# Attention pieces spaced 10 and 18 instead of 14, inverse columns counted at 3.0 instead of 4.5, and MoE 1's low parts on GpSimd

## The chip, the cores and the metric

The kernel runs on one core of a Trainium2 chip. Its five engines have queues of their own that run in order: TensorE (PE, with weight loads listed apart as PEld), VectorE (DVE), ScalarE (ACT), GpSimd (POOL) and SyncE (SP), which issues transfers. An instruction that waits for a semaphore holds up all that stands behind it on its engine. The metric is the device time of one execution in microseconds, lower is better.

## The reference

Three stages follow each other: a delta-rule attention, a MoE layer without a nonlinearity (a product of two projections), and a second layer with a leaky ReLU of learned slope. All is in float32.

```python
# attention: 4 batches x 8 heads, 768 steps, head size 48
k_n = k / (norm(k) + 1e-06)
for t in range(S):
    y[:, :, t] = einsum('bhd,bhde->bhe', q[:, :, t], state)
    v_old = einsum('bhde,bhd->bhe', state, kt)
    state = state + bt * einsum('bhd,bhe->bhde', kt, vt - v_old)
# x: 3072 tokens x 384
x = ((x @ w_a) * (x @ w_b)) @ w_out                      # MoE 1, d_ff 1536
h = x @ w_in                                             # MoE 2, d_ff 2048
out = (maximum(h, 0) + alpha * minimum(h, 0)) @ w_out2
```

## The kernel before, in words

**Attention** is done in six chunks of 128 time steps (`c` = 0 to 5), each in two halves of 64 (`j`). Within a chunk the recurrence is solved by inverting a triangular matrix for each of 32 (half, head pair) tiles. VectorE does that inverse by substitution: it transposes the matrix (line 287), then adds thirty *columns*, two instructions each, a multiply into `itmp` (line 303) and an add into `eu` (line 304). Each column needs the one before it. The result is transposed twice at the start of the chunk that uses it: into `hw` (line 311) and into `TT` (line 315), and ScalarE copies part of TT (line 319).

On TensorE a chunk is a series of *pieces*. First three pieces of `offdiag` (products `w` and `xx`, lines 337 and 353, kept by ScalarE into `hw` and `TT`), then for each half `step`: two each of `rp`, `up`, `sp` and `yp`. Beside the `up` and `sp` pieces of the first half stand the key products of the *next* chunk (line 220, "mates", whose result VectorE masks into `ef`, line 253), and beside those of the second half its query products. When the last key product is masked, behind the second `sp` of the first half, `keys_done` begins the next chunk's inverse. It goes on in the background and has to be finished before the next chunk's first piece, since `w` reads `hw`.

**MoE 1** of chunk c - 1 fills TensorE between the pieces of chunk c. It is a generator (`moe1`) that yields once for each 128x128x512 product, 324 steps a chunk: up projections `p` (line 640) into two banks, whose product `a` (line 595) VectorE forms, and down projections `o` (line 642). For accuracy each float32 operand is *split* into a high part (a ScalarE cast, line 538) and a low part (a subtraction, line 539), and each product is made of three passes. The weight of a step (`wu`) is split shortly ahead of use by `prepare`, three ahead; the low part goes to VectorE or GpSimd by a string, `LO` while weights are still being decoded, `STEADY` afterwards and `LAST` once MoE 2's weights are being decoded. The low parts of `g` are always GpSimd's (line 604).

**The order** is written out by the program as it is built. `run(moe, n, start)` puts n MoE steps between two pieces and moves a count `now` on by one a step, and by `PIECE` = 5 for the piece. `FILLS[c]` is that n. The inverse goes on through `leisurely`: it puts the next column into VectorE's queue whenever VectorE's booked time `until[DVE]` has been reached by `now`; each column books 4.5 + (31 - m) m / 100 counts (line 298; 1.7 in place of 4.5 for chunk 1's inverse, which lies in PSUM). What has not been placed by the end of the chunk is placed at once by `finish(inv)`, behind the splits of `x`, the chunk's result. So these counts decide only in which order instructions stand in a queue; on the chip each waits for what it needs.

After the last `yp` of a chunk the MoE steps are run down to 16, the result is transposed and split into `x` (lines 458 and 539), 10 more steps end the chunk's MoE, and the next chunk starts with 17 steps beside the two transposes (`DIAGONAL` = 8, 4, 5).

Chunk 0 runs before MoE 1 starts. In chunk 1 MoE 1's weights are decoded from the form in which they arrive, on all of ScalarE, VectorE and GpSimd (lines 500 to 510). Chunk 5 has no next inverse; there, from its first `rp` on, MoE 2's weights are decoded. After chunk 5 the rest of MoE 1 runs, then MoE 2.

Of the kernel before, what the change touches and what calls it, by code (L numbers as in the profile page):

```python
# [22 lines left out]
ACT, DVE, POOL, SP = "act", "dve", "pool", "sp"  # L23
# [5 lines left out]
SLACK = 0.5  # L29

PIECE = 5
FILLS = (0, 13, 14, 14, 14, 14)

AHEAD, WAIT = 6, 21
DIAGONAL = (8, 4, 5)
# [23 lines left out]
XAHEAD = 32  # L59


LO = "ppppppv"
STEADY = "ppppv"
LAST = "ppv"

STAGES = [("u", 4), ("g", 2), ("r", 2), ("w6", 1), ("w7", 1), ("w8", 1)]
# [14 lines left out]
class Attention:  # L81
# [198 lines left out]
    def inverting(s, L, room=None):  # L280

        nc, ap = s.nc, s.ap
        a0 = ap.tile([128, 32, 32], F32, tag="eu", name="eu", bufs=1)
        nc.vector.transpose(a0, L["ef"][:, :, 0:32].rearrange("p a t -> p t a"))
        s.spend(DVE, 9)
        yield
        nc.vector.memset(a0.rearrange("p t s -> p (t s)")[:, 0:1024:33], 1.0)  # L290
        eu = L["eu"] = a0
        if room is not None:
            eu = L["eu"] = room
            nc.scalar.copy(eu, a0)
        yield
        tmp = ap.tile([128, 256], F32, tag="itmp", name="itmp", bufs=1)
        for m in range(1, 31):
            s.spend(DVE, (1.7 if room is not None else 4.5) + (31 - m) * m / 100)
            nt = 31 - m
            a = eu[:, m : m + 1, 0:m].to_broadcast([128, nt, m])  # L300
            b = a0[:, m + 1 : 32, m : m + 1].to_broadcast([128, nt, m])
            tm = tmp[:, : nt * m].rearrange("p (t s) -> p t s", s=m)
            nc.vector.tensor_tensor(tm, a, b, ALU.mult)  # L303
            nc.vector.tensor_tensor(eu[:, m + 1 : 32, 0:m], eu[:, m + 1 : 32, 0:m], tm, ALU.add)  # L304
            yield
# [160 lines left out]
def attn_moe_kernel(tc, kt, qt, kn, vn, beta, w_a, w_b, w_o, w_in, w_o2, alpha, out):  # L466
    nc = tc.nc
    with ExitStack() as ctx:
# [13 lines left out]
        def bank(name, tag):  # L482
            return pools[tag].tile([128, 512], F32, tag=tag, name=name, bufs=BANKS[tag])
# [49 lines left out]
        def xroom(kk, c, shape, dt, name):  # L533
            return xp.tile([128, *shape], dt, tag=f"x{kk}{c % 2}", name=name)

        def split(dst, src, eng=nc.gpsimd):

            nc.scalar.copy(dst[:, 0], src)  # L538
            eng.tensor_tensor(dst[:, 1], src, f32(dst[:, 0]), ALU.subtract)  # L539
            spend(ACT, 2)  # L540
            if eng is nc.vector:
                spend(DVE, 2.2)
            else:
                spend(POOL, 4.5)
# [20 lines left out]
        def prepare():  # L565
# [3 lines left out]
            if m is not None:  # L569
# [3 lines left out]
                ready.append(gp.tile([128, 2, DM], F32R, tag="u", name="wu", bufs=NU))  # L573
                lo = LO if left or line else STEADY
                if len(wanted) < 2 * M2:
# [96 lines left out]
        def run(it, n, start=0):  # L672

            nonlocal now
            more = True
            now += start
            for _ in range(n):
                more = more and next(it, "end") is None
                now += 1
                for b in list(background):  # L680
                    if next(b, "end") == "end":
                        background.remove(b)
            return more

        def leisurely(inv):

            while True:
                if until[DVE] <= now and next(inv, "end") == "end":
                    return
                yield  # L690

        def finish(b):
            for _ in b:
                pass
            background[:] = [x for x in background if x is not b]
# [23 lines left out]
        room = p0.tile([128, 32, 32], F32, tag="inv", name="inv")  # L719
# [71 lines left out]
        def decoding(depth):  # L791
            while left or line:
                decode1(depth)
                yield
# [34 lines left out]
        def decoding2(depth):  # L829
            while wanted or line:  # L830
                rooms = spare if len(wanted) <= len(spare) else free
                if len(wanted) > keep[0] and rooms and len(line) < depth:
                    begin(line, weight2(*wanted.pop(0), rooms.pop(0)))
                else:
                    advance(line)
                yield
# [59 lines left out]
        moe = moe1()  # L896
        for c in range(NSC):

            going = c > 0
            fill = FILLS[c]  # L900
            if c > 0:
                N = A.load(c + 1) if c + 1 < NSC else None
                if c == 1:
                    finish(inv)
                    diagonal = A.diagonal(L)
                    now = max(now, until[DVE])
                    background.append(decoding(DEPTH))
                    run(moe, WAIT)
                    for _ in diagonal:
                        run(moe, 1)  # L910
                    early_ctx.close()
                    pools["out"] = ctx.enter_context(tc.tile_pool(name="psm", bufs=1, space=PSUM))
                    going = run(moe, AHEAD) and going
                else:
                    for n, _ in enumerate(A.diagonal(L)):
                        run(moe, DIAGONAL[n])
                tag = "chain" if c == 1 else "pre"
                for i, _ in enumerate(A.offdiag(L, tag)):
                    going = run(moe, fill, PIECE) and going
                    if N is not None:  # L920
                        if i == 1:
                            norms = A.norms(N)
                        if i > 0:
                            next(norms)
                mates = [[None, None], [None, None]]

                def keys_done():
                    nonlocal inv
                    A.fold(N, 1)
                    inv = A.inverting(N)  # L930
                    background.append(leisurely(inv))
                    A.scale_keys(N)

                if N is not None:
                    after = {(0, 8): lambda: A.fold(N, 0), (1, 8): keys_done}
                    for q in range(2):
                        mates[q] += [A.mate(N, *jg, tag, q == 1, after.get(jg) if q == 0 else None, c > 1) for jg in HALF]
                closed.clear()
                L["y"] = [None, None]
                for j in range(2):  # L940
                    for i, _ in enumerate(A.step(c, j, L, mates[j])):
                        if N is not None and i == j == 0:
                            next(norms, None)
                            A.masks(N, 0)
                            A.masks(N, 1)
                        going = run(moe, fill, PIECE) and going
                        if c == NSC - 1 and i == j == 0:
                            rooms2.append(rooms1.pop())
                            background.append(decoding2(DEPTH2))
                        if N is not None and i == 3:  # L950
                            A.load_values(c + 1, N)
                    keep[0] = 2 * M2 - KEEP
                    if N is not None and j == 0:
                        A.scale_values(N, 0)
                if N is not None:
                    A.scale_values(N, 1)
                while togo[0] > AHEAD1:
                    run(moe, 1)
                X[c] = []
                for kk in range(KT):  # L960
                    X[c].append(xroom(kk, c, [2, 512], F32R, "x"))
                    split(X[c][-1], A.transposed(L["y"], kk, xp=bank("xp", "pre" if kk == 2 else "chain")), nc.vector)
                    run(moe, min(2, togo[0]))
                run(moe, togo[0])
                if N is not None:
                    finish(inv)
            else:
                x1 = [bank("x1", "ab") for _ in range(2)]
                for kk in range(KT):
                    at = kk % 2 * 256  # L970
                    A.transposed(L["y"], kk, (1,), x1[kk // 2], at)
                    split(xs[kk][:, :, 256:], x1[kk // 2][:, at : at + 256], nc.vector)
                while len(ready) < LEAD:
                    prepare()
            L = N
# [53 lines left out]
        going, ahead = True, XAHEAD - 3  # L1029
        while going or background:  # L1030
            going = run(moe, 9)
# [96 lines left out]
```

## Time and profile before

| | us |
|---|---|
| median of 3 runs | 1156.25 (1155.47 to 1157.4) |
| profiled execution | 1155.86, of which span 1154.1 |
| TensorE busy | 1048.2 (91%) |
| VectorE busy | 672.7 (58%) |
| GpSimd busy | 555.9 (48%) |
| ScalarE busy | 467.3 (40%) |
| chain that ended last | TensorE 69%, VectorE 16%, ScalarE 6%, GpSimd 4% |

The stages, in us from the start of the span: chunk 0 and its preparation to about 110, chunk 1 to 235, chunks 2, 3, 4 and 5 at some 109 each (their first `w` at 242.5, 351.4, 460.3 and 568.8), the rest of MoE 1 to 745, MoE 2 to the end at full speed of TensorE. Busy shares over the whole span hide that the stages have different limits: VectorE is busy 7 tenths of the time up to 670 and 4 tenths behind it. What a chunk is worth is read inside the chunk.

### The profile page before, as it was taken

How to read it: one execution, taken by the hardware profiler on the slowest of the kernel's cores; microseconds unless marked ns; L12 is line 12 of the kernel's file. 1: busy time of each engine (PE TensorE's matmuls, PEld its weight loads, DVE VectorE, ACT ScalarE, POOL GpSimd, SP SyncE). 2: the span in 40 equal slices, each digit the busy share in tenths (PEclk: the TensorE clock that was granted, in tenths of full speed). 3: DMA queues.
4: the chain of work that ended last, by engine and by line, in shares of the span. 5: the costliest groups of instructions: out<-in, count | busy, mean ns of one | idle time of the engine just before them, and what ended most of it. 6: DMA issues, size and time to landing. Idle time of an engine off the chain costs nothing.

```text
span 1154.1 us, 23828 instructions
## 1 busy us (share of the span) xinstructions
PE 1048.2 (91%) x10048; PEld 885.1 (77%) x10048; DVE 672.7 (58%) x1085; ACT 467.3 (40%) x903; POOL 555.9 (48%) x467
## 2 busy tenths in 40 slices
PE   6277898779998997999799999999999999999997
PEld 5165686567776776777677887799999999999997
DVE  7787577755774579468737468734343433434332
ACT  4273664554345433643456577511221121122211
POOL 6255588736463644554447678632223333333222
PEclk8577998889998999999899999999999999999999
DMA  9215132500030021000024144010202001020101
GB/s 266 79 30 165 52 108 64 151 29 16 15 83 29 16 66 33 30 16 15 4 75 119 39 137 133 24 50 1 56 1 55 1 8 48 1 56 1 28 1 28
DMA packets 25596, 61.42 MB, mean 53 GB/s; under 512 B 4496, under 2 KB 7568, under 8 KB 25488
## 3 DMA queue, kind: packets, MB, share of 16 engines
q1 hardware_dynamic: 25168, 59.50, 17.8%
q8 instruction: 79, 1.29, 0.5%
q10 hardware_dynamic: 320, 0.39, 0.1%
q14 instruction: 29, 0.24, 0.1%
HBM read 50.44 MB, written 9.44 MB: 52 GB/s over the span
## 4 chain that ended last, share of the span: by engine, by line
PE 69%; DVE 16%; ACT 6%; POOL 4%; issue 3%; DMA 1%; ACTq 0%; POOLq 0%; DVEq 0%
PE h L551 17%; PE p L640 17%; PE o L1009 17%; PE o L642 10%; DVE itmp L303 4%; DVE eu L304 2%; DVE inv L304 1%; PE rp L408 1%; PE yp L447 1%; DVE v L827 1%; PE up L421 1%; POOL W L510 1%; DVE hw L311 1%; ACT wu L538 1%; PE g L220 1%
## 5 line engine op out<-in xcount | busy, mean ns | idle before, releaser
L640 PE MATMUL p<-x,wu 128*128 128x512 f32 x1296 | 332.5, 401 | 11.4 <-DVE a L595 6.3
L640 PEld LDWEIGHTS p<-x,wu 128*128 128x128 f32 x1296 | 241.3, 191 | 67.0 <-issue 7.9
L539 POOL TENSOR_TENSOR wu<-W,wu 128x384 fp32r<-128x384 f32 x166 | 177.7, 1074 | 203.6 <-ACT wu L538 186.1
L539 POOL TENSOR_TENSOR g<-neg,g 128x512 fp32r<-128x512 f32 x95 | 123.2, 1297 | 276.8 <-ACT g L538 276.8
L1009 PE MATMUL o<-v,g 128*128 128x384 f32 x1152 | 217.8, 337 | 0.2 <-ACT g L538 0.2
L551 PE MATMUL h<-x,v 128*128 128x512 f32 x864 | 215.2, 393 | 0.0
L1009 PEld LDWEIGHTS o<-v,g 128*128 128x128 f32 x1152 | 204.6, 188 | 9.2 <-ACT g L538 0.6
L1000 DVE TENSOR_SCALAR neg<-h,al 128x512 f32<-128x512 f32 (+1 forms) x97 | 72.3, 745 | 218.1 <-PE h L551 217.3
L538 ACT CAST g<-neg 128x512 fp32r<-128x512 f32 (+1 forms) x97 | 59.7, 615 | 325.6 <-DVE neg L1001 315.5
L551 PEld LDWEIGHTS h<-x,v 128*128 128x128 f32 x864 | 160.7, 188 | 29.3
L642 PE MATMUL o<-g,wu 128*128 128x512 f32 x648 | 178.7, 412 | 1.3 <-DVE TT L315 0.6
L642 PEld LDWEIGHTS o<-g,wu 128*128 128x128 f32 x648 | 124.4, 197 | 30.1 <-DVE wu L539 1.0
L538 ACT CAST wu<-W 128x384 fp32r<-128x384 f32 x216 | 108.7, 512 | 46.8 <-POOL W L510 23.4
L604 POOL TENSOR_TENSOR g<-a,g 128x512 fp32r<-128x512 f32 x71 | 95.4, 1344 | 40.8 <-ACT g L599 40.8
L595 DVE TENSOR_TENSOR a<-p,a 128x512 f32<-128x512 f32 x72 | 49.4, 686 | 65.3 <-PE p L640 29.4
L539 DVE TENSOR_TENSOR wu<-W,wu 128x384 fp32r<-128x384 f32 x50 | 52.0, 1040 | 59.6 <-ACT wu L538 58.3
L599 ACT CAST g<-a 128x512 fp32r<-128x512 f32 x72 | 44.5, 618 | 84.6 <-DVE a L595 84.3
L220 PE MATMUL g<-Z 48*64 48x64 f32 x768 | 61.8, 241 | 13.8 <-DMA Z<-in_kt_dram 7.0
L304 DVE TENSOR_TENSOR eu<-eu,itmp 128x30 f32<-128x30 f32 (+14 forms) x120 | 68.9, 575 | 4.1
L1001 DVE SCALAR_TENSOR_TENSOR neg<-h,neg 128x512 f32<-128x512 f32 (+1 forms) x97 | 66.5, 686 | 3.3
L220 PEld LDWEIGHTS g<-Z 48*64 48x64 f32 x768 | 55.9, 153 | 14.7 <-DMA Z<-in_kt_dram 6.8
L303 DVE TENSOR_TENSOR itmp<-eu 128x30 f32<-128x30 f32 (+14 forms) x120 | 65.3, 544 | 2.8
(101 smaller groups left out, 1284.6 us busy)
## 6 DMA issues: line engine op xcount, KB each, us to landing
v<-in_w_in_dram SPq DMA_DIRECT2D x16, 384.0 KB, 3.4
v<-in_w_o_dram SPq DMA_DIRECT2D x16, 384.0 KB, 3.8
k<-in_kn_dram SPq DMA_DIRECT2D x6, 768.0 KB, 5.0
Z<-in_kt_dram SPq DMA_DIRECT2D x24, 192.0 KB, 5.8
Z<-in_qt_dram SPq DMA_DIRECT2D x24, 192.0 KB, 6.7
v<-in_vn_dram SPq DMA_DIRECT2D x12, 384.0 KB, 3.3
raw<-in_w_a_dram SPq DMA_DIRECT2D x12, 384.0 KB, 5.7
raw<-in_w_b_dram SPq DMA_DIRECT2D x12, 384.0 KB, 6.1
```

Of the source, the lines that this page charges most:

```text
L220: nc.tensor.matmul(g[0:64, i, :], Z[64:112, 0, i8 + i, :], Z[64:112, a, i8 + i, :], start=True, stop=True)
L303: nc.vector.tensor_tensor(tm, a, b, ALU.mult)
L304: nc.vector.tensor_tensor(eu[:, m + 1 : 32, 0:m], eu[:, m + 1 : 32, 0:m], tm, ALU.add)
L538: nc.scalar.copy(dst[:, 0], src)
L539: eng.tensor_tensor(dst[:, 1], src, f32(dst[:, 0]), ALU.subtract)
L551: nc.tensor.matmul(p, u[:, a, kk * 128 : kk * 128 + 128], xs[kk][:, b], start=(n == 0), stop=(n == 3 * KT - 1))
L604: (nc.vector if last else nc.gpsimd).tensor_tensor(g[m][:, 1], a[m], f32(g[m][:, 0]), ALU.subtract)
L640: nc.tensor.matmul(ab[m, t], wu, X[c][kk][:, q], start=(n == 0), stop=(n == 8))
L642: nc.tensor.matmul(o[kk], wu, g[m][:, q], start=(m == 0 and n < 3), stop=(m == M1 - 1 and n > 5),)
L1000: nc.vector.tensor_scalar(t[:, cs], h[:, cs], 0.0, al[:, m : m + 1], ALU.min, ALU.mult)
L1001: nc.vector.scalar_tensor_tensor(t[:, cs], h[:, cs], 0.0, t[:, cs], ALU.max, ALU.add)
L1009: nc.tensor.matmul(o[n], g[:, a, n * 128 : n * 128 + 128], V[m][1][:, b], start=(m == 0 and i == 0), stop=(m == M2 - 1 and i == 2),)
```

## The change

Four numbers and two strings are altered.

- `FILLS` has two numbers for each chunk. The first is the number of MoE steps behind the three `offdiag` pieces and the first six pieces of half 0 (`rp`, `up`, `sp`, two each), that is until the next inverse begins; the second stands behind all later pieces. Chunks 2 to 4 had 14 throughout and now have 10 and 18; chunk 1 had 13 and has 11 and 14; chunk 5 had 14 and has 13 and 14.
- A column of an inverse in SBUF books 3.0 instead of 4.5 counts (plus the same second term).
- `LO` and `STEADY` are "p": every low part of MoE 1's weights is GpSimd's until `LAST` applies. VectorE has 21 low parts of `wu` instead of 50.

```diff
-FILLS = (0, 13, 14, 14, 14, 14)
+FILLS = ((0, 0), (11, 14), (10, 18), (10, 18), (10, 18), (13, 14))
...
-LO = "ppppppv"
-STEADY = "ppppv"
+LO = "p"
+STEADY = "p"
 LAST = "ppv"
...
         for m in range(1, 31):
-            s.spend(DVE, (1.7 if room is not None else 4.5) + (31 - m) * m / 100)
+            s.spend(DVE, (1.7 if room is not None else 3.0) + (31 - m) * m / 100)
...
-            fill = FILLS[c]
+            fill, fill2 = FILLS[c]
...
-                        going = run(moe, fill, PIECE) and going
+                        going = run(moe, fill if j == 0 and i < 6 else fill2, PIECE) and going
```

VectorE's queue at the end of chunk 2, before. The rows are the last columns that stand ahead of the splits of `x`, the splits, and the first of nine columns behind them; `hw` follows behind the ninth.

```order
L595 TENSOR_TENSOR a<-p,a 128x512
L303 TENSOR_TENSOR itmp<-eu 128x220
L304 TENSOR_TENSOR eu<-eu,itmp 128x11x20
L303 TENSOR_TENSOR itmp<-eu 128x210
L304 TENSOR_TENSOR eu<-eu,itmp 128x10x21
L539 TENSOR_TENSOR x<-xp,x 128x512 x3
L595 TENSOR_TENSOR a<-p,a 128x512
L539 TENSOR_TENSOR wu<-W,wu 128x384
L303 TENSOR_TENSOR itmp<-eu 128x198
L304 TENSOR_TENSOR eu<-eu,itmp 128x9x22
```

The same place in VectorE's queue now:

```order
L303 TENSOR_TENSOR itmp<-eu 128x58
L304 TENSOR_TENSOR eu<-eu,itmp 128x2x29
L303 TENSOR_TENSOR itmp<-eu 128x30
L304 TENSOR_TENSOR eu<-eu,itmp 128x30
L595 TENSOR_TENSOR a<-p,a 128x512
L539 TENSOR_TENSOR x<-xp,x 128x512 x3
L595 TENSOR_TENSOR a<-p,a 128x512
L311 STREAM_TRANSPOSE hw<-eu 128x32x32
L315 STREAM_TRANSPOSE TT<-eu 128x32x32
```

The column of 30 is the last one. It now stands ahead of `x`, in chunks 3 and 4 too; in chunk 1 three columns still stand behind `x`, where there were eleven.

ScalarE's queue at the start of chunk 2, before, from the copies of TT to the second copies of `hw`:

```order
L319 COPY TT<-TT 32x32x32
L592 COPY a<-p 128x512
L319 COPY TT<-TT 32x32x32
L342 COPY hw<-w 32x512 x2
L538 CAST wu<-W_543 128x384
L599 CAST g<-a 128x512
L651 COPY x2s<-o_2896 128x512
L651 COPY x2s<-o_2897 128x512
L651 COPY x2s<-o_2898 128x512
L538 CAST wu<-W_555 128x384
L342 COPY hw<-w 32x512 x2
```

And now:

```order
L319 COPY TT<-TT 32x32x32
L592 COPY a<-p 128x512
L319 COPY TT<-TT 32x32x32
L342 COPY hw<-w 32x512 x2
L538 CAST wu<-W_543 128x384
L599 CAST g<-a 128x512
L651 COPY x2s<-o_2896 128x512
L651 COPY x2s<-o_2897 128x512
L651 COPY x2s<-o_2898 128x512
L342 COPY hw<-w 32x512 x2
L358 COPY TT<-xx 32x16x32 x2
```

One weight cast has moved behind the second copies of `hw`; the rest of the stretch is the same.

## Rows read from the trace of the kernel before

**Rows 1.** Busy time by stage (chunk 1, chunk 2); columns as its first line.
```profile
core 0: us, PE busy (x) PEld busy (x) DVE busy (x) ACT busy (x) POOL busy (x), PEclk, DMA share, GB/s
121.00:232.00 111.00, 94.73 (x1117) 73.58 (x1116) 78.87 (x134) 64.82 (x131) 82.58 (x73) 0.92 0.33 97
341.00:450.00 109.00, 101.85 (x1361) 81.84 (x1360) 73.75 (x122) 47.86 (x92) 53.61 (x45) 0.97 0.14 38
```

**Rows 2.** TensorE in order of time: start, us, what, [idle before, releaser]; four `w`.
```profile
242.51 0.71 PE L337 MATMUL w<-hw,ef 32*32 32x32 f32 x19 [7.42 <-DVE hw L311]
...
351.44 1.92 PE L337 MATMUL w<-hw,ef 32*32 32x32 f32 x64 [7.15 <-DVE hw L311]
...
460.34 0.28 PE L337 MATMUL w<-hw,ef 32*32 32x32 f32 x3 [6.98 <-DVE hw L311]
...
568.79 0.34 PE L337 MATMUL w<-hw,ef 32*32 32x32 f32 x5 [6.36 <-DVE hw L311]
```

**Rows 3.** TensorE in order of time, pieces that follow boundaries 1, 2 and 4.
```profile
258.08 0.25 PE L408 MATMUL rp<-SU,Z 48*64 48x48 f32 x1
...
358.02 0.22 PE L353 MATMUL xx<-TT,hw 32*32 32x32 f32 x2
...
362.63 1.20 PE L353 MATMUL xx<-TT,hw 32*32 32x32 f32 x64
363.76 2.33 PE L642 MATMUL o<-g,wu 128*128 128x512 f32 x9
...
367.16 0.25 PE L408 MATMUL rp<-SU,Z 48*64 48x48 f32 x1
...
585.04 0.25 PE L408 MATMUL rp<-SU,Z 48*64 48x48 f32 x1
```

**Rows 4.** VectorE in order of time, boundary 2.
```profile
338.96 0.68 DVE L595 TENSOR_TENSOR a<-p,a 128x512 f32<-128x512 f32 x1
...
349.27 2.02 DVE L311 STREAM_TRANSPOSE hw<-eu 128x1024 f32<-128x1024 f32 x1
351.14 1.90 DVE L315 STREAM_TRANSPOSE TT<-eu 128x1024 f32<-128x1024 f32 x1
```

**Rows 5.** VectorE in order of time, boundary 1 and boundary 3.
```profile
229.74 0.68 DVE L595 TENSOR_TENSOR a<-p,a 128x512 f32<-128x512 f32 x1
...
238.87 0.25 DVE L303 TENSOR_TENSOR itmp<-eu 128x84 f32<-128x84 f32 x1
...
240.39 1.97 DVE L311 STREAM_TRANSPOSE hw<-eu 128x1024 f32<-128x1024 f32 x1
...
449.62 0.67 DVE L595 TENSOR_TENSOR a<-p,a 128x512 f32<-128x512 f32 x1
```

**Rows 6.** ScalarE in order of time, start of chunk 2.
```profile
353.07 1.04 ACT L319 COPY TT<-TT 32x1024 f32<-32x1024 f32 x1 [8.63 <-DVE TT L315]
...
355.69 1.18 ACT L342 COPY hw<-w 32x512 f32<-32x512 f32 x2
...
359.94 1.17 ACT L342 COPY hw<-w 32x512 f32<-32x512 f32 x2
...
367.14 0.23 ACT L169 ACTIVATE s<-ss 128x32 f32<-128x32 f32 x1
```

**Rows 7.** VectorE and GpSimd in order of time, two column multiplies in chunk 2.
```profile
435.75 0.40 DVE L303 TENSOR_TENSOR itmp<-eu 128x240 f32<-128x240 f32 x1
...
436.62 1.25 DVE L303 TENSOR_TENSOR itmp<-eu 128x238 f32<-128x238 f32 x1
...
436.59 1.01 POOL L539 TENSOR_TENSOR wu<-W,wu 128x384 fp32r<-128x384 f32 x1 [1.18 <-ACT wu L538]
```

**Rows 8.** The page's groups: low parts of MoE 1's weights; busy, mean ns, idle before.
```profile
L539 POOL TENSOR_TENSOR wu<-W,wu 128x384 fp32r<-128x384 f32 x166 | 177.7, 1074 | 203.6 <-ACT wu L538 186.1
...
L539 DVE TENSOR_TENSOR wu<-W,wu 128x384 fp32r<-128x384 f32 x50 | 52.0, 1040 | 59.6 <-ACT wu L538 58.3
```

**Rows 9.** Who waited for whom, 112 to 235 us: total, times, longest.
```profile
ACT wu L538 <- POOL W L510: 23.4, 12, 3.9
...
PE up L421 <- DVE ef L253: 2.3, 1, 2.3
```

## The prediction

> **What bounds the kernel now.** I first read the busy times by stage [rows 1]: in the stretch of one attention chunk with its MoE 1 (109 us) TensorE is busy 101.9 us, VectorE 73.8, GpSimd 53.6, ScalarE 47.9. So TensorE sets the time, and what is to be had are its pauses. Listing TensorE's rows in order of time, I find between 232 and 709 us just four pauses that matter, each in front of the first product of a new chunk (`w`, line 337), each ended by the VectorE transpose `hw` (line 311): 7.42, 7.15, 6.98 and 6.36 us, together 27.9 us [rows 2]. I call these boundaries 1 to 4 (chunks 1 to 4 handing over to 2 to 5).
>
> Each pause costs a second time. After it the granted clock is at the lower of its two levels, 1.2 GHz (mean 0.97 over the stage, [rows 1]), and the same work is slower. At boundary 2, `w` to the next `rp` took 367.16 - 351.44 = 15.72 us [rows 2, 3]. At full clock this is: a piece of 64 small products 363.76 - 362.63 = 1.13, 14 MoE steps 367.16 - 363.76 = 3.40, the doubled piece with 14 steps 362.63 - 358.02 = 4.61, then 1.13 and 3.40 again: 13.67. So 2.05 us are lost. Boundary 1 loses 258.08 - 242.51 - 13.67 = 1.90, boundary 4 585.04 - 568.79 - 13.67 = 2.58; the third I put between, at 2.2. Sum 8.7. The Trainium skill ("TensorE: Matmul & The Clock Gate", its table of terms) reckons such a penalty as the throttled time times the share withheld: from the mean clock that is 109 x 0.03 = 3.3 us a boundary instead of 2.05, and the forecast would be some 4 us lower. I use the rows, because part of the throttled time is the pause itself.
>
> Why is `hw` late? VectorE is in arrears with the inverse's columns: at boundary 2 it has finished `x` and the product `a` at 338.96 + 0.68 = 339.64, and starts `hw` only at 349.27 [rows 4]. The 9.63 us between hold nine columns, a low-part split and its wait.
>
> **The change, part by part.** Durations and the sum are those of the profiled run: 1155.86 us, of which 1154.1 span; the median of the runs shown is 1156.25, so 0.4 is added at the end.
>
> *Pieces and columns.* One MoE step is 3.40 / 14 = 0.243 us with its share of changeovers [rows 3]. From the inverse's first transpose to `x` VectorE had 14 x 10 + 39 = 179 steps; it now has 10 + 18 x 9 + 39 = 211, so 32 x 0.243 = 7.8 us more. The steps of a chunk stay 324, so this room is taken from the stretch before the inverse, at no cost by itself. Five low-part splits leave VectorE in that stretch, 5 x 1.04 = 5.2 us [rows 8]. Relief 13.0 against arrears of 9.6; and the new order has all thirty columns of chunks 2 to 4 ahead of `x`. Then `hw` starts behind `a`: at 339.64, ends at 339.64 + 2.02 = 341.7 [rows 4], while TensorE comes to `w` at 351.44 - 7.15 = 344.3. That is 2.6 us to spare; at boundary 3, with `a` ending at 450.29 and TensorE there at 453.36, still 1.1 [rows 2, 5]. At boundary 1 three short columns stay behind `x`: 240.39 - 238.87 = 1.52, so 230.42 + 1.52 + 1.97 = 233.9 against 242.51 - 7.42 = 235.1, 1.2 to spare [rows 2, 5]. All four pauses should go, and with them the low clock: -27.9 - 8.7.
>
> *GpSimd against VectorE.* A column's multiply of 128x240 took 0.40 us with GpSimd idle, and one of 128x238 took 1.25 where it began while a 1.01 us split ran on GpSimd [rows 7]. Five more splits there can hold columns by at most 5 x 1.07 = 5.4 us [rows 7, 8]. With that, 13.0 + 2.6 - 9.6 - 5.4 = 0.6 us remain: it just fits. The Trainium skill ("SBUF — State Buffer", section "SBUF: two separate sides") states this as a rule: a VectorE instruction with two inputs in SBUF and a GpSimd one take one pair of ports in turn, "the other fully blocks". The trace agrees (1.25 against 0.40). By the rule at its worst boundary 1, with four splits, would be 4 x 1.07 - 1.2 = 3.1 us late and lose 1.9 in clock: 5 us more than my sum.
>
> *What is late next.* The pieces after `w` now come after 10 steps, 2.43 us, not 3.40. ScalarE needs 3.80 us from its first TT copy to the end of the `hw` copies (353.07 to 356.87) [rows 6]. Free of its earlier work at 353.07 - 8.63 = 344.44, and with TT done at 341.66 + 1.90 = 343.56, it finishes `hw` at 348.24. TensorE comes to the doubled piece at 344.29 + 1.13 + 2.43 = 347.85: a wait of 0.4. The second `hw` copies end 361.11 - 356.87 = 4.24 later, at 352.5 (a weight cast has moved out from between, so rather 352.0); TensorE comes at 348.24 + 1.22 + 2.43 = 351.9 (1.22 is 4.61 less 14 steps): 0.1 to 0.6. I take 0.7 a boundary, 2.8 in all; bounds 0 and the 3.3 a boundary of the second rival. The other nearer pieces (`rp`, `up`, `sp`) are three steps of 2.43 plus 1.1 apart from what they need, more than any wait the rows show there.
>
> *Chunk 1*, where weights are also decoded, is the unclear part: TensorE is idle 111.0 - 94.7 = 16.3 us in it [rows 1], partly on queues that wait for GpSimd (ScalarE 23.4 us for its decoded weights, [rows 9]). Four splits move onto that queue, 4 x 1.07 = 4.3 at most; six stretches before the second `up` lose 2 steps each as cover, 12 x 0.243 = 2.9, where 2.3 are waited for now [rows 9]. These 7.2 are the upper end; the lower end is -16.3, if all its stalls went. I take +2.5, near the row of 2.3, since GpSimd has 28 us of idle time there. Chunk 5 has one step less in nine stretches and no inverse; TensorE is never idle in it behind boundary 4, so 0. The MoE 2 part is not touched. In SyncE's queue two loads of values change places with one weight load each: 0, since values are first read four pieces later.
>
> Sum: 1155.9 - 27.9 - 8.7 + 2.8 + 2.5 = 1124.6; with 0.4 for the median **1125**. Its own range is 1117 to 1131.
>
> **Rivals.**
> *First boundary stays.* In chunk 1 eight more columns must fit before `x`, among the decode's instructions. If they don't, or GpSimd's splits hold them, the pause of 7.4 and its 1.9 return: 1134. For it: VectorE's 79 busy us of 111 [rows 1] and the port rows [rows 7]; against: 32 idle us, and four splits less.
> *ScalarE takes over.* Its copies from TT to the last `hw` and TT occupied it without a pause from 353.07 to 367.37, 14.3 us [rows 6]; TensorE now offers 11.0 from `w` to `rp` (three pieces of 3.5, ten steps each 2.43). If nothing of it slips behind, 3.3 us a boundary are waited for, and the low clock stays (8.7): 1125 + 4 x 2.6 + 8.7 = 1144. Against: its last copies are needed only at `up`, two pieces later.
> *It does not do what it says.* The columns are planned earlier but VectorE still reaches `hw` late, since its lateness came from GpSimd's port and not from the plan: 1150 to 1158. Against: the sum of 13.0.
> *Slower.* The pieces before the inverse are a chain through one buffer (bank "pre": `up` and `sp` share it with the next chunk's key products, which VectorE must read out, after GpSimd's masks, each time). If four of these waited 2.3 us each, like the one in chunk 1 [rows 9], each followed by the low clock (2.2), a chunk would pay 4 x 4.5 = 18; chunks 2 to 4 54, against 31 gained: 1178. It decides from 10 us a chunk. Against: in the same chunks none of these waits exists at 14 steps.
>
> **Chances.** The forecast 0.60; better, through fewer stalls in chunk 1 (1110 to 1117), 0.04; first boundary 0.13; ScalarE 0.12; no effect 0.05; slower 0.06. The range, 1116 to 1143, holds the first three and part of the fourth. About 0.2% is what a measurement of this kernel can tell from no change: faster by more 0.90, within 0.03, slower 0.07.
>
> **What would show it.** Right: no wait of `w` for `hw` above 1 us at boundaries 2 to 4; the last column ahead of `x`; the granted clock at its full level from chunk 2 to the end of MoE 1; a chunk of 101 us instead of 109; short waits of `xx` for ScalarE's `hw`. Wrong: TensorE waiting for VectorE or ScalarE at `up` or `sp` of chunks 2 to 4; weights (`wu`) waited for by TensorE on GpSimd; chunk 1 longer by more than 7 us.

## The result and the profile after

The changed kernel takes 1127.76 us in the median (1127.51 to 1127.9, 4 runs), before 1156.09 in the same comparison: a ratio of 0.9753, 95% interval 0.9736 to 0.977. The forecast was 1125, its range 1116 to 1143. The profiled execution took 1127.51 us, of which 1125.8 span.

The page of the kernel after: busy time, share of the span and instructions of three engines, and the granted clock in 40 slices.

```profile
span 1125.8 us, 23835 instructions
...
PE 1046.4 (93%) x10048; PEld 882.6 (78%) x10048; DVE 679.1 (60%) x1056; ACT 464.6 (41%) x903; POOL 582.3 (52%) x496
...
PEclk8566998899999999999999999999999999999999
```

TensorE's work is the same, its pauses are fewer. VectorE is busier than before in sum, although 29 low parts have left it: that is the first surprise, and it comes back below.

TensorE of the kernel after in order of time, the four places of [rows 2]: start, us, what, and the idle time before where there was some.

```profile
236.42 0.25 PE L337 MATMUL w<-hw,ef 32*32 32x32 f32 x5 [1.03 <-DVE hw L311]
...
339.94 0.24 PE L337 MATMUL w<-hw,ef 32*32 32x32 f32 x3
...
441.24 0.24 PE L337 MATMUL w<-hw,ef 32*32 32x32 f32 x3
...
542.54 0.24 PE L337 MATMUL w<-hw,ef 32*32 32x32 f32 x3
```

Of 27.9 us in front of `w` 1.0 is left, all of it at boundary 1. Busy time by stage shows the clock too (columns as in [rows 1]; chunks 1 to 4, the windows moved with the stages):

```profile
121.00:228.00 107.00, 88.92 (x1026) 67.86 (x1024) 87.83 (x137) 59.46 (x122) 81.79 (x72) 0.92 0.29 90
228.00:331.00 103.00, 100.23 (x1348) 79.99 (x1349) 76.91 (x121) 47.08 (x92) 61.24 (x53) 0.98 0.20 51
331.00:432.00 101.00, 100.23 (x1360) 80.17 (x1359) 73.60 (x112) 48.11 (x94) 62.15 (x53) 1.00 0.14 41
432.00:533.00 101.00, 100.25 (x1361) 80.09 (x1360) 73.61 (x112) 48.12 (x95) 62.15 (x53) 1.00 0.06 18
```

In chunks 3 and 4 TensorE is busy 100.2 of 101 us at the full granted clock, so little is left in its pauses there. In chunk 2 it was at the lower level for a while. At boundary 1 `w` still waits 1.03 us, and one piece later TensorE waits again, for ScalarE's copies:

```profile
241.39 0.24 PE L353 MATMUL xx<-TT,hw 32*32 32x32 f32 x2 [1.24 <-ACT hw L342]
...
242.00 0.21 PE L353 MATMUL xx<-TT,hw 32*32 32x32 f32 x1 [0.36 <-ACT hw L342]
```

What made `hw` late there, at the end of chunk 1: TensorE's transpose of the result, then VectorE from the product `a` behind `x` to `hw` (the add is that of the last of the three columns behind `x`), and the GpSimd split beside the add:

```profile
228.14 0.66 PE L458 MATMUL xp<-ident,y 128*128 128x128 f32 x4 [2.77 <-DVE raw L507]
...
231.21 0.68 DVE L595 TENSOR_TENSOR a<-p,a 128x512 f32<-128x512 f32 x1
...
233.09 1.00 DVE L304 TENSOR_TENSOR eu<-eu,itmp 128x30 f32<-128x30 f32 x1
234.12 2.15 DVE L311 STREAM_TRANSPOSE hw<-eu 128x1024 f32<-128x1024 f32 x1
...
233.03 1.01 POOL L539 TENSOR_TENSOR wu<-W,wu 128x384 fp32r<-128x384 f32 x1 [1.69 <-ACT wu L538]
```

VectorE at boundary 2, to be held against [rows 4]:

```profile
329.37 0.19 DVE L304 TENSOR_TENSOR eu<-eu,itmp 128x30 f32<-128x30 f32 x1
329.48 0.68 DVE L595 TENSOR_TENSOR a<-p,a 128x512 f32<-128x512 f32 x1
332.64 0.69 DVE L539 TENSOR_TENSOR x<-xp,x 128x512 fp32r<-128x512 f32 x1 [2.48 <-ACT x L538]
...
335.34 2.25 DVE L311 STREAM_TRANSPOSE hw<-eu 128x1024 f32<-128x1024 f32 x1
337.48 2.02 DVE L315 STREAM_TRANSPOSE TT<-eu 128x1024 f32<-128x1024 f32 x1
```

The last column ends 3.1 us before the first split of `x`, VectorE then waits 2.48 us for `x`, and `hw` is done at 337.59, 2.35 us before TensorE comes at 339.94. Predicted were 2.6. ScalarE behind it, as in [rows 6]:

```profile
340.07 1.04 ACT L319 COPY TT<-TT 32x1024 f32<-32x1024 f32 x1
...
342.68 1.18 ACT L342 COPY hw<-w 32x512 f32<-32x512 f32 x2
...
346.53 1.17 ACT L342 COPY hw<-w 32x512 f32<-32x512 f32 x2
```

From the first copy of TT to the end of the `hw` copies it is 3.79 us (3.80 before), so the first `xx` waits there. From `w` to the first `rp` TensorE took 351.38 - 339.94 = 11.44 us at boundary 2, 11.48 at boundary 3, 13.00 at boundary 4 and 14.49 at boundary 1. One new wait in chunks 3 and 4 is not ScalarE's; in chunk 3:

```profile
362.29 0.50 PE L642 MATMUL o<-g,wu 128*128 128x512 f32 x1 [0.59 <-POOL wu L539]
```

The time from the first `w` of a chunk to that of the next, as differences of their starts in the traces (us; in the last column the first `w` of chunk 5 to the start of MoE 2), with all experiments. Each row is one profiled execution. Up to boundary 2 the program of e10 is that of the changed kernel, and its chunks 1 and 2 are 0.97 us longer and 0.83 shorter; smaller differences there say nothing.

```
kernel                    chunk 1  chunk 2  chunk 3  chunk 4  chunk 5 and rest
before                     132.71   108.93   108.90   108.45   175.13
after                      126.96   103.52   101.30   101.30   172.73
e1  spacing only           136.61   106.55   106.63   106.24   175.18
e2  count only             135.40   108.69   108.04   104.49   173.71
e3  low parts only         131.25   105.97   105.96   105.48   174.81
e4  all but spacing        128.84   104.02   101.99   101.89   173.68
e5  all but count          131.06   102.69   102.36   102.38   173.59
e6  all but low parts      135.71   103.05   103.68   105.16   172.76
e7  all, 5 kept in chunk 1 136.18   102.90   101.30   101.30   172.88
e9  e6, VectorE no wait    132.79   103.71   101.15   101.92   172.90
e10 one more transpose     127.93   102.69   103.04   103.59   174.09
e12 copies behind hw       126.23   101.96   101.95   101.95   172.80
e13 e7, five left out      131.44   102.86   101.30   101.30   172.88
e14 e12, chunk 1 at 13     128.28   101.99   101.94   101.95   172.81
```

### The profile page after: what moved, and what is told of

It reads as the page before. It is cut to its first block, busy times and chain, and to the rows that moved or that the text cites. A ratio compares the mean times of both kernels' runs of the same rounds, so it can differ in the third digit from the quotient of the medians.

```text
span 1125.8 us, 23835 instructions
## 1 busy us (share of the span) xinstructions
PE 1046.4 (93%) x10048; PEld 882.6 (78%) x10048; DVE 679.1 (60%) x1056; ACT 464.6 (41%) x903; POOL 582.3 (52%) x496
## 4 chain that ended last, share of the span: by engine, by line
PE 71%; DVE 11%; ACT 8%; POOL 5%; issue 4%; DMA 1%; ACTq 0%; POOLq 0%; DVEq 0%
PE p L640 19%; PE h L551 18%; PE o L1009 18%; PE o L642 9%; DVE itmp L303 2%; DVE inv L304 1%; PE yp L447 1%; PE rp L408 1%; ACT wu L538 1%; POOL W L510 1%; DVE v L827 1%; PE g L220 1%; PE up L421 1%; POOL wu L539 1%; ACT hw L342 1%
## 5 line engine op out<-in xcount | busy, mean ns | idle before, releaser
L640 PE MATMUL p<-x,wu 128*128 128x512 f32 x1296 | 338.8, 406 | 8.2 <-ACT a L592 5.1
L539 POOL TENSOR_TENSOR wu<-W,wu 128x384 fp32r<-128x384 f32 x195 | 205.7, 1062 | 166.3 <-ACT wu L538 154.0
L642 PE MATMUL o<-g,wu 128*128 128x512 f32 x648 | 170.7, 401 | 2.5 <-POOL wu L539 1.1
L642 PEld LDWEIGHTS o<-g,wu 128*128 128x128 f32 x648 | 121.7, 191 | 31.7 <-POOL wu L539 2.8
L304 DVE TENSOR_TENSOR eu<-eu,itmp 128x30 f32<-128x30 f32 (+14 forms) x120 | 85.4, 711 | 4.1
L303 DVE TENSOR_TENSOR itmp<-eu 128x30 f32<-128x30 f32 (+14 forms) x120 | 83.3, 694 | 2.9
L220 PE MATMUL g<-Z 48*64 48x64 f32 x768 | 62.2, 242 | 16.1 <-DMA Z<-in_kt_dram 6.7
L221 PE MATMUL g<-Z 48*64 48x64 f32 x768 | 61.6, 242 | 3.4 <-issue 2.2
```

What stands on the lines that cost most here:

```text
L220: nc.tensor.matmul(g[0:64, i, :], Z[64:112, 0, i8 + i, :], Z[64:112, a, i8 + i, :], start=True, stop=True)
L640: nc.tensor.matmul(ab[m, t], wu, X[c][kk][:, q], start=(n == 0), stop=(n == 8))
L642: nc.tensor.matmul(o[kk], wu, g[m][:, q], start=(m == 0 and n < 3), stop=(m == M1 - 1 and n > 5),)
```

## The experiments

The prediction's sum takes the pauses away by two terms, the spacing and the low parts' move, and has none for the columns' count. Three doubts stood against it: that the count alone was at fault, that a low part moved to GpSimd costs a held-up column as much as it saves, and where chunk 1's gain came from. The edits are to the changed kernel, so that an experiment on one part alone sets the two others back; `...` stands for lines left out. Ratios are to the kernel before.

**e1, the spacing alone.** The count is 4.5, `LO` and `STEADY` as before.

```diff
-LO = "p"
-STEADY = "p"
+LO = "ppppppv"
+STEADY = "ppppv"
...
-            s.spend(DVE, (1.7 if room is not None else 3.0) + (31 - m) * m / 100)
+            s.spend(DVE, (1.7 if room is not None else 4.5) + (31 - m) * m / 100)
```

> Only the spacing of the pieces is changed; columns are counted 4.5 and the low parts are shared as before. In the order of this kernel 8, 5, 4 and 5 columns stand behind x at boundaries 1 to 4. Theory A (room: VectorE is short of time between the inverse's begin and x, and the 32 steps, 7.8 us, are what relieves it): pauses of some 4.5 us at boundary 1 and 0 to 2 at the others, 1132 to 1140 us. Theory B (the count: VectorE has time enough, columns are only placed too late): nine columns become four or five, so pauses of 1 to 3 us each and most of the low clock stay: 1140 to 1148 us.

1152.76 us, ratio 0.9954 (0.9938 to 0.9971): worse than either theory. Who waited for whom, from 200 to 600 us (total, times, longest):

```profile
PE w L337 <- DVE hw L311: 17.0, 4, 6.4
```

At boundaries 2 to 4 the pauses fell from 7.15, 6.98 and 6.36 to 4.19, 2.92 and 3.42, by 3.3 on average and not by 7.8; chunk 1 became 3.9 us longer.

**e2, the count alone.**

```diff
-FILLS = ((0, 0), (11, 14), (10, 18), (10, 18), (10, 18), (13, 14))
+FILLS = ((0, 0), (13, 13), (14, 14), (14, 14), (14, 14), (14, 14))
...
-LO = "p"
-STEADY = "p"
+LO = "ppppppv"
+STEADY = "ppppv"
```

> Only the columns' count is changed (3.0); 14 steps between pieces and low parts as before. 8, 4, 4 and 3 columns stand behind x. Theory B (the count): four or fewer columns are 2 us and boundaries 2 to 4 have 1 to 2.6 us to spare, so only boundary 1 keeps a pause: 1132 to 1138 us. Theory A (room): VectorE had 6.7 us of idle time in that stretch of chunk 2 before, against arrears of 9.6, so it fills up and still reaches the transpose late by some 3 us at each boundary, with part of the low clock: 1140 to 1148 us.

1151.2 us, 0.9944 (0.9929 to 0.9958). Both theories miss. With three or four columns left behind `x`, worth 2 us, the pauses should have vanished if only the order mattered; at boundaries 2 to 4 they are 5.25, 3.69 and 1.27:

```profile
PE w L337 <- DVE hw L311: 15.1, 4, 5.3
```

**e3, the low parts alone.**

```diff
-FILLS = ((0, 0), (11, 14), (10, 18), (10, 18), (10, 18), (13, 14))
+FILLS = ((0, 0), (13, 13), (14, 14), (14, 14), (14, 14), (14, 14))
...
-            s.spend(DVE, (1.7 if room is not None else 3.0) + (31 - m) * m / 100)
+            s.spend(DVE, (1.7 if room is not None else 4.5) + (31 - m) * m / 100)
```

> Only the low parts are changed: all of MoE 1's weights by GpSimd until the last stage. 10, 6, 6 and 6 columns stand behind x. As predicted (VectorE is relieved of 5.2 us a chunk): pauses fall by about 4 us each, 1136 to 1145 us. Port theory (each split on GpSimd holds up a column for as long as VectorE saves: with the whole change the columns took 168.7 us in place of 134.2, and the splits on VectorE 25.6 in place of 52.0): pauses as long as before, 1152 to 1160 us.

1144.15 us, 0.9884 (0.9869 to 0.9899): as predicted in the whole, and the port theory falls. But the relief is smaller than 5.2:

```profile
PE w L337 <- DVE hw L311: 18.3, 4, 6.4
```

The pauses are 3.96, 4.00 and 3.99 us at boundaries 2 to 4, so 2.8 us less on average.

**e6, all but the low parts.**

```diff
-LO = "p"
-STEADY = "p"
+LO = "ppppppv"
+STEADY = "ppppv"
```

> The whole change but for the low parts, which are shared as before. 5, 0, 0 and 0 columns stand behind x. As predicted (5.2 us of relief a chunk is missing): VectorE reaches the transposes 2 to 4 us later, pauses of 1 to 2 us, 1131 to 1138 us. Port theory: columns are shorter again (134 to 145 us in all), nothing is lost at boundaries 2 to 4, and chunk 1 keeps two more columns behind x: 1125 to 1130 us.

1142.65 us, 0.9874 (0.9859 to 0.9889). Both theories miss: `w` waits at boundary 1 alone (4.2 us), so at boundaries 2 to 4 `hw` is in time without the low parts' move, yet 14.9 us are lost against the whole change, 8.8 of them in chunk 1 and 6.2 in chunks 3 and 4. In chunks 3 and 4 TensorE loses them further on, at the first `xx` behind boundary 2 and at a product in chunk 4 that needs VectorE's `Z`:

```profile
353.47 0.24 PE L353 MATMUL xx<-TT,hw 32*32 32x32 f32 x2 [1.28 <-ACT hw L342]
...
526.11 0.24 PE L220 MATMUL g<-Z 48*64 48x64 f32 x1 [2.20 <-DVE Z L270]
```

The granted clock was at its lower level for a while after each (0.86 of full on average from 353 to 365 us, 0.72 from 525 to 531). The groups of columns and of VectorE's low parts in this kernel (busy, mean ns, idle before):

```profile
L304 DVE TENSOR_TENSOR eu<-eu,itmp 128x30 f32<-128x30 f32 (+14 forms) x120 | 78.6, 655 | 4.1
L303 DVE TENSOR_TENSOR itmp<-eu 128x30 f32<-128x30 f32 (+14 forms) x120 | 66.9, 557 | 2.4
L539 DVE TENSOR_TENSOR wu<-W,wu 128x384 fp32r<-128x384 f32 x50 | 54.6, 1092 | 68.1 <-ACT wu L538 68.0
```

The last of these groups in chunk 1 alone (110 to 240 us):

```profile
L539 DVE TENSOR_TENSOR wu<-W,wu 128x384 fp32r<-128x384 f32 x5 | 5.0, 1002 | 11.1 <-ACT wu L538 11.1
```

The five low parts there take 5.0 us, but VectorE stands 11.1 us in front of them, waiting for a cast, with columns and decoding queued behind. The same groups after:

```profile
L304 DVE TENSOR_TENSOR eu<-eu,itmp 128x30 f32<-128x30 f32 (+14 forms) x120 | 85.4, 711 | 4.1
L303 DVE TENSOR_TENSOR itmp<-eu 128x30 f32<-128x30 f32 (+14 forms) x120 | 83.3, 694 | 2.9
L539 DVE TENSOR_TENSOR wu<-W,wu 128x384 fp32r<-128x384 f32 x21 | 25.6, 1220 | 24.5 <-ACT wu L538 23.3 <-POOL f L510 1.2
```

So the move takes 29.0 us of work and 43.6 us of waiting off VectorE, and puts 23.2 us onto its columns. This led to the next three.

**e7, chunk 1 keeps its low parts** (`LO` "ppppppv", `STEADY` "p").

```diff
-LO = "p"
+LO = "ppppppv"
```

> The whole change, but while weights are still decoded (chunk 1) VectorE keeps one low part in seven. If the low parts' gain lies in chunk 1, as the stage times of the kernel without them say (135.7 us from w to w against 127.0 with them), this run has 134 to 136 us in chunk 1 and 101 to 103 in chunks 2 to 4: 1134 to 1138 us. If it lies in chunks 2 to 4, where I predicted it (5.2 us a chunk), chunk 1 takes 127 to 129 us and the whole 1127 to 1131.

1136.25 us, 0.9815 (0.9802 to 0.9829): five low parts in chunk 1 are 8.5 us. Chunk 1 takes 136.2, chunks 3 and 4 101.30 as in the changed kernel. I had costed them as a loss for GpSimd.

**e9, nearly the same work without the wait.** Based on e6 (`LO` and `STEADY` as there); VectorE's low parts read a constant.

```diff
...
-            eng.tensor_tensor(dst[:, 1], src, f32(dst[:, 0]), ALU.subtract)
+            if still:
+                i3 = A.ident.unsqueeze(1).to_broadcast([128, 3, 128])
+                eng.tensor_tensor(dst[:, 1].rearrange("p (n q) -> p n q", q=128), i3, i3, ALU.subtract)
+            else:
+                eng.tensor_tensor(dst[:, 1], src, f32(dst[:, 0]), ALU.subtract)
...
+                v = lo[turns % len(lo)] == "v"
+                split(ready[-1], W[m][i], nc.vector if v else nc.gpsimd, v and lo != LAST)
```

> The low parts are shared as before, but VectorE's (those before MoE 2's weights are decoded) subtract a constant from itself in place of the weight's high part from the weight: the same shape with two inputs in SBUF, without the wait for ScalarE's cast and for GpSimd's decode; these low parts are zero, so the output differs. Everything else is the whole change. Waiting theory (the low parts cost VectorE their place in its queue: 68.0 us of idle time in front of 50 of them): chunk 1 falls from 135.7 to 127 to 130 us, the whole to 1128 to 1133 us. Busy theory (they cost what they take, 1.09 us each): chunk 1 stays at 134 to 136 us, the whole at 1140 to 1143.

1133.81 us, 0.9796 (0.9783 to 0.981). Of the 14.9 us of e6, 8.8 go with the wait: chunks 3 and 4 are back at 101.2 and 101.9, and chunk 1 fell by 2.9 of 8.8. The work is not quite the same, since a low part here takes 0.84 us and the same 29 in e6 took 1.00 ((54.6 - 25.6) / 29); that is 4.6 us of VectorE's time in all, and how much of it is in the 8.8 was not separated. The busy theory falls; the waiting theory holds in chunks 3 and 4 and for a third of chunk 1.

```profile
L541 DVE TENSOR_TENSOR wu<-ident 128x384 fp32r<-128x384 f32 x29 | 24.4, 842 | 8.3 <-PE p L645 5.2 <-PE o L647 1.8 <-POOL wu L543 1.3
```

**e13, e7 with the five left out.**

```diff
...
+            if still:
+                eng.memset(f32(dst[:, 1]), 0.0)
+                spend(ACT, 2)
+                spend(DVE, 2.2)
+                return
```

> As the run in which chunk 1 keeps one low part in seven on VectorE, but these five are left out: VectorE writes zeros there, without input, so the output differs, and GpSimd does not do them either. If what counts is VectorE's time in chunk 1 (its wait and its work, 136.2 us with the five low parts on it, 127.0 with them on GpSimd), chunk 1 takes 125 to 128 us, the whole 1126 to 1129. If GpSimd pays for them as I predicted (4.3 us at most), chunk 1 is shorter than the changed kernel's by 2 to 4 us: 1123 to 1126. If neither counts and only the order did, chunk 1 stays above 131.

1131.94 us, 0.9781 (0.9767 to 0.9794); chunk 1 takes 131.44, 4.7 less than with them and 4.5 more than in the changed kernel. By the number the third expectation (above 131) came out, narrowly. The 4.5 are not VectorE's load: it is busy 96.1 us in chunk 1 here and 99.4 in the changed kernel. The bookings for the five low parts are kept, so five columns stand behind `x` and not three, and the pause before `w` is as long as in e7:

```profile
PE w L337 <- DVE hw L311: 4.7, 1, 4.7
```

So of the 9.2 us that e7 loses in chunk 1 about half goes with the parts' work and waiting, and half stays with the places in the order. Of this second half 3.7 us are the longer pause (4.7 for 1.0); the rest was not separated. e9, with the work and without the wait, takes 132.79 us in chunk 1, 1.4 more than this run, so by these two runs the work is the smaller part there too.

**e10, `hw` transposed twice at boundaries 2 to 4.**

```diff
+        s.times = 1
...
-        nc.vector.transpose(hw.rearrange("p a s -> p s a"), eu.rearrange("p t s -> p s t"))
+        for _ in range(s.times):
+            nc.vector.transpose(hw.rearrange("p a s -> p s a"), eu.rearrange("p t s -> p s t"))
...
+            A.times = 2 if c > 2 else 1
```

> The whole change, with the transpose into hw done twice at boundaries 2 to 4, so hw and TT are ready 2.1 us later. By the prediction's slack at w (2.6, 1.1 and 2.6 us; 339.94 less 337.59 = 2.4 in the trace of the changed kernel) nothing is lost: within 1 us of the changed kernel. Rival, ScalarE's chain: its copies of TT start only 0.5 us after TT is done and the first xx piece already waits 0.3 for the hw copies behind them, so each boundary is 1.5 to 1.9 us longer: 4 to 6 us more, 1132 to 1134.

1133.17 us, 0.9791 (0.9778 to 0.9805), 5.4 us more than the changed kernel: the rival is right. No `w` waits more than 0.06 us at boundaries 2 to 4, so the 2.35 us there were real and covered it; the first `xx` waits instead, here at boundary 2 (the edit moves the line numbers by two):

```profile
345.17 0.24 PE L355 MATMUL xx<-TT,hw 32*32 32x32 f32 x2 [1.28 <-ACT hw L344]
345.77 0.21 PE L355 MATMUL xx<-TT,hw 32*32 32x32 f32 x1 [0.36 <-ACT hw L344]
```

**e12, ScalarE's copies of TT behind its first `hw` copies.** The two copies leave `diagonal` and stand in `offdiag`:

```diff
-        for sl in (slice(0, 32), slice(64, 96)):
-            yield
-            nc.scalar.copy(TT[sl, :, 0:32], TT[sl, :, 32:64])
-            s.spend(ACT, 4.5)
+        yield
+        yield
...
         for i in range(16):
             products(i)
         keep()
+        for sl in (slice(0, 32), slice(64, 96)):
+            nc.scalar.copy(TT[sl, :, 0:32], TT[sl, :, 32:64])
+            s.spend(ACT, 4.5)
         yield
```

> The whole change, with ScalarE's two copies of TT put behind its first copies of hw (they are needed only by the piece after). If ScalarE's chain is what TensorE waits for at the first xx (1.24 and 0.36 us with the low clock at boundary 1, 0.34 and 0.15 at 2 and 3), these waits go: 2 to 5 us less, 1123 to 1126 us. If the copies are only moved in front of the next wait (second hw copies, third piece), the time is the same within 1 us.

1125.09 us, 0.972 (0.9707 to 0.9733), the fastest of all, faster than the changed kernel by 2.7 us with intervals that just part. The first theory has the number, and both are half right in kind. The gain is from chunk 0 to chunk 1 (64.04 us from `w` to `w`, 65.50 after) and in chunk 2 (101.96 for 103.52); the waits in front of the first `w` of chunks 1 and 2 fall from 0.94 and 1.03 us to 0.25 and none. At boundaries 1 to 3 the wait has moved to the third piece, 1.05 us each, and chunks 3 and 4 are 0.65 us longer. That wait at boundary 1 (the edit moves the line numbers):

```profile
242.76 1.20 PE L351 MATMUL xx<-TT,hw 32*32 32x32 f32 x64 [1.05 <-ACT hw L340]
```

**e4, all but the spacing** (`FILLS` 13 in chunk 1, 14 elsewhere, as in e2).

> The whole change but for the spacing, which is as before (13 in chunk 1, 14 elsewhere). 5, 1, 1 and 1 columns stand behind x. Room theory: in the changed kernel VectorE has no pause from the inverse's begin to the last column, which ends 2.5 us before the first split of x; 32 steps (7.8 us) less, and less the 2.5 and some 2.4 to spare at w, leave it 3 us late at each of boundaries 2 to 4: 104 to 106 us a chunk, 1135 to 1142 us. Count theory (the order is what matters, one column is 0.5 us): chunks 2 to 4 stay at 101 to 102, and chunk 1, where the closer pieces cost 3.9 us by themselves, gains: 1125 to 1130 us.

1131.85 us, 0.9784 (0.977 to 0.9797). The room theory falls in chunks 2 to 4: with the count and the low parts VectorE is in time at 14 steps too, and 0.6 to 0.7 us in each of chunks 3 and 4 is all that the spacing adds there. The count theory is wrong on chunk 1, 1.9 us longer instead of shorter, with 4.7 us waited for at boundary 1, the only one where `w` waits:

```profile
PE w L337 <- DVE hw L311: 4.7, 1, 4.7
```

**e5, all but the count** (4.5 again, as in e1).

> The whole change but for the columns' count, which is 4.5 again. 7, 2, 2 and 2 columns stand behind x. If only the order counts: two short columns are 0.9 us and within what is to spare at w, but TT comes as much later for ScalarE's chain, so 0.5 to 1 us a chunk at 2 to 4; at boundary 1 four more columns are 3 us and the low clock: 1131 to 1135 us. If spreading the columns also frees VectorE for chunk 1's decode (the count alone made chunk 1 2.7 us longer), chunk 1 gains that back: 1127 to 1131 us.

1133.73 us, 0.9798 (0.9784 to 0.9811), as the first theory had it: `w` waits 5.1 us at boundary 1 and not at the others, and chunks 3 and 4 are 1.1 us longer, with waits of 0.9 and 0.36 us at the first `xx` of boundaries 2 and 3.

```profile
PE w L337 <- DVE hw L311: 5.1, 1, 5.1
```

**e14, e12 with chunk 1 at 13 steps** (`FILLS[1]` = (13, 13)).

> The copies of TT behind the first hw copies, and chunk 1's pieces 13 steps apart as before, all else as changed. Four columns stand behind x at boundary 1. The closer pieces alone made chunk 1 3.9 us longer, so without them: 2 to 4 us less than with the copies moved alone, 1121 to 1123 us. Rival: the column more behind x and the later begin of the inverse bring the pause at boundary 1 back by 1 to 3 us with the low clock: 1125 to 1129.

1126.27 us, 0.9733 (0.9719 to 0.9746), the rival: chunk 1 takes 128.3 and not 126.2, and `w` waits 1.7 us at boundary 1.

```profile
PE w L335 <- DVE hw L311: 1.7, 1, 1.7
```

## Why the prediction was right

**The pauses and the clock: right.** 26.9 of 27.9 us went, and with them the low clock at boundaries 2 to 4. The size of the clock's share can be checked in chunk 3, which fell by 108.90 - 101.30 = 7.60 us. The pause was 6.98, the clock 2.05 by the rows, and new waits take 0.69 (11.44 from `w` to `rp`, where the prediction's terms at full clock give 13.67 - 12 x 0.243 = 10.75) and 0.59 (a weight on GpSimd): 7.75 expected. By the page of the Trainium skill that I weighed ("TensorE: Matmul & The Clock Gate", its table of terms), with its estimate of 3.3 in place of 2.05, it would have been 9.0. The rows were nearer: before, the granted clock averaged 0.85 of full already in the pause at boundary 2 (344.3 to 351.4 us), where there was nothing to slow down. Not as said: the clock was at its lower level once in chunk 2 (243.6 to 247.1 us) and once behind chunk 5, after a wait of 1.83 us at 682.69.

**What relieves VectorE: right in sum, by luck, and wrong in its terms.** This is the step that failed. I wrote "Relief 13.0 against arrears of 9.6", 7.8 from the spacing and 5.2 from the low parts, and gave the count no term. At boundaries 2 to 4 each part alone shortens the pause, 6.8 us on average, by 3.3 (spacing), 3.4 (count, the mean of 1.9, 3.3 and 5.1) and 2.8 us (low parts), and any two of the three clear it (e4, e5, e6). The parts help each other: at boundary 2 the spacing alone takes away 3.0 us and the count alone 1.9, both together 7.1. VectorE's idle time from the inverse's first column to `x`, in chunks 2 to 4, fits this. Before it was 8.1 to 10.2 us. The spacing alone leaves 7.7 to 9.1, so the old count places the columns too late to use the time; the count alone leaves 2.9 to 3.9, so there it is time that is short.

**GpSimd against VectorE: the price was right, the gain was mis-sized.** I allowed 5.4 us a chunk for columns held up; the columns took 134.2 us before and 168.7 after, of which the low parts' move is 23.2 (e6 to after), 5.8 a chunk. But what VectorE gained was not only the 1.04 us of a low part's work: the row that I quoted, [rows 8], has 59.6 us of idle time in front of 50 of them, 1.2 us each, and I priced the work alone. With that wait removed, and little else, the kernel gains 8.8 us (e9).

**Chunk 1: right by luck.** From `w` to `w` I expected -7.4 + 2.5 = -4.9; it was -5.75. The terms are others. The low parts (five, where I counted four) that I booked as a loss of up to 4.3 for GpSimd are a gain of 8.5 in the whole change (e7), though only 1.5 us by themselves (e3), and the closer pieces and the count, alone, make the chunk 3.9 and 2.7 us longer. GpSimd did have the idle time that I took for the middle: 31.8 us in chunk 1 after.

**What is late next: right at two boundaries of four.** ScalarE's `hw` copies are what TensorE meets next: 0.7 us at boundaries 2 and 3, as predicted, and e10 shows that there is no room in that chain. At boundary 4 next to nothing is lost (13.00 us from `w` to `rp`, 12.94 by the terms): chunk 5's pieces are 13 steps apart, and I had reckoned with 10. At boundary 1 it is 14.49 - 10.75 = 3.7 us, the waits of 1.24 and 0.36 and the low clock.

The forecast is 2.7 us too low, and chunk 2 alone is 2.9 off: it fell by 5.4 us where the sum has 1.9 + 7.15 - 0.7 = 8.35. Chunks 3 and 4 are 0.7 off each, mostly by the wait for a weight on GpSimd that the sum does not have; chunk 1 and the stretch from chunk 5 on came out better than the sum by 0.8 and 0.5 and cover them, so that the total is as near as this is luck in part. In e10, with the same program up to there, chunk 2 falls short by 2.1 and chunk 1 by 0.1. In both runs boundary 1 is the main miss. I had 1.2 us to spare there, with `hw` done at 233.9 and TensorE coming at 235.1. TensorE came at 235.39, but `hw` was done at 236.27. Of the 2.4 us 1.5 are the product `a`, which ended at 231.89 and not at 230.42, behind a result that TensorE transposed later (it waits 2.77 us for VectorE's decode in front of that, 0.84 before). Another 0.8 are the last column's add, which took 1.00 us beside a GpSimd split and 0.19 before.

**The rivals.** The one with the first boundary left standing came about in small, in part for a reason that it gives (a GpSimd split); ScalarE taking over is real, at 0.7 us a boundary in place of 3.3 and without the low clock at boundaries 2 to 4; the two others (no effect, slower) have nothing for them: no piece before the inverse waits at 10 steps but for 0.6 us on a weight behind GpSimd's masks, which the prediction lists among the signs of being wrong.

## What to carry to other kernels

In an in-order queue an instruction costs its work and the wait in front of it, so read both numbers of its group before moving it; here the wait was the larger part (8.8 of 14.9 us went with it). Where several parts of a change feed the same arrears, don't price each by itself and add: a queue that is late needs time, things to do in that time, and no blocked head. Here each part alone took some half of the pause, and any two took all of it. A pause that is removed has the next one right behind it, and one added transpose tells how far.

## What the runs showed of the hardware

A column's two-input instructions run at two speeds. In the kernel after 130 of the 240 ran beside a GpSimd instruction for more than 30% of their time and took 1.02 us on average, the other 110 took 0.33; before it was 96 at 0.92 and 144 at 0.32. Before, 79 of the 240 began while GpSimd was at work, and all 68 that took over 0.7 us are among them; after, all 111 of that length are among 119. The "SBUF — State Buffer" page of the Trainium skill (section "SBUF: two separate sides") has this as one of the two waiting for the whole instruction of the other, which these times fit.

Short waits of TensorE were followed by its lower clock in some places and not in others. At boundary 1 after, a wait of 1.03 us and one of 1.24 some 5 us later were followed by 1.2 GHz, as every single pause of 6.4 to 7.4 us was before. In e10 waits of 1.28 and 0.36 us at boundary 2 left it at 2.4 GHz, and nearly the same pair at boundary 3 (1.26 and 0.36) did not; e12, with three waits of 1.05 us and one of 1.90, stayed at 2.4 GHz. The mean granted clock, as a share of 2.4 GHz, is the third number from the right; two stretches of e10, then one of e12:

```profile
345.00:356.00 11.00, 10.40 (x251) 8.41 (x252) 1.52 (x2) 9.66 (x17) 4.29 (x4) 1.00 0.21 74
448.00:459.00 11.00, 10.44 (x245) 8.23 (x246) 1.49 (x2) 9.68 (x17) 4.22 (x4) 0.84 0.21 74
232.00:1100.00 868.00, 858.51 (x7376) 727.42 (x7375) 487.41 (x693) 337.62 (x659) 426.49 (x356) 1.00 0.13 39
```

What decides between them no run here shows.
